# Fewer warm-up products, ScalarE's conversion steps queued behind relus, and the last bank scaled from PSUM

## The chip, the core and the metric

The kernel runs on one NeuronCore of a Trainium2 chip. Five engines each work through an instruction stream of their own, in order: TensorE (PE, with its weight loads shown as PEld), VectorE (DVE), ScalarE (ACT), GpSimd (POOL) and SyncE (SP), which here only issues transfers. They wait for each other by semaphores. The metric is the device time of one execution in microseconds.

## What is computed

Attention over 8 batches, 8 heads, 576 positions and 64 columns per head, with a threshold below the maximum, and then a feed-forward block on the result with a residual:

```python
scores = scale * np.matmul(q, k.transpose(0, 1, 3, 2))
thresh = np.max(scores, axis=-1, keepdims=True) - tau
scores = np.where(scores >= thresh, scores, -1000000000.0)
attn = np.exp(scores - np.max(scores, axis=-1, keepdims=True))
attn = attn / (np.sum(attn, axis=-1, keepdims=True) + 1e-09)
x = np.matmul(attn, v)            # then heads side by side: (8, 576, 512)
mu = np.mean(x, axis=-1, keepdims=True)
var = np.mean((x - mu) ** 2, axis=-1, keepdims=True)
xn = (x - mu) / np.sqrt(var + 1e-06) * g_ln
out = x + np.maximum(xn @ w_ch1, 0.0) @ w_ch2
```

w_ch1 (512 by 2048) and w_ch2 (2048 by 512) come as 64-bit floats, read by the kernel as 64-bit integers; q, k and v are 32-bit floats.

## The kernel before

**Slots.** The attention runs in slots n = 0, 1, ...: nine to a batch (SLOTS), four head pairs by the first 256 query columns, one for the last 64 columns of all heads, four more head pairs. In a slot PE makes the scores (L413) in two banks groups sc0 and sc1; DVE takes the negated maxima (L427), POOL the thresholds (L431), ACT the exponentials (L441, two per bank group), DVE compares, masks and sums (L448). In batch 0 ACT makes diagonal matrices of the reciprocals (L462) and PE turns the weights with them (tp, tr), copied to SBUF by ACT as em and er (L498, L521); from batch 1 on POOL divides (L464), DVE transposes 32 by 32 blocks into et (L538), and SP stores them to a scratch (scr) and reads them back turned. PE multiplies with v (L596, L606), ACT copies to x (L619), POOL sums features (L648). DVE also turns q and k of the slot ahead (turn, L364 to L374), after POOL has scaled q (L360).

**The feed-forward block** has 16 groups g of 288 tokens. Its steps are a generator that is advanced in the four quarters of each slot by `second_part`, which deals PE work by a count of what is owed until the next group. `first_part` computes 16 tiles of hidden units (d = 0 to 15): four products of two halves each into a bank p1, then a relu on ACT (L790). There are two banks for p1 and everything else in that pool, so tile d + 2 waits for the relu of tile d. Meanwhile ACT squares the centred input (L796), POOL adds the four parts (L798), PE multiplies the sum for the variance, and ACT takes log and exponential for the reciprocal root (L806 to L808); DVE refines it (L731 to L735). Group 0 then goes through `second_plain`: for each m = 0 to 3, sixteen products and a copy by ACT (L828). The later groups go through `second_quarters`, seven segments of products on halves of the tokens and of the hidden units, whose banks ACT copies out (L877), and DVE or POOL adds (L881), multiplies by the root and adds x (`finish`, L889 and L881).

**The order is written out by hand.** No scheduler moves instructions: the program order of each engine is the order of the calls. Calls meant for a later place are kept in lists (aside, stores, drops, at_quarter).

**The weights' conversion.** Class `Weights` takes 32 chunks of 128 by 512 (512 KB as 64-bit): 16 of w_ch1, then 16 of w_ch2. SP fetches a chunk into free room (L255). `begin` issues two DVE steps (L274, L278) and two ACT steps (L282 on the low words, L286 squares the high words). `carry` is an integer add on POOL that needs L282 and L278 (L292). `mask` is a DVE step (L301) that needs the carry and L286. `scale` multiplies a chunk of w_ch1 by g on POOL (L313). The first part may not use a tile of w_ch1 until its chunks have been scaled, the second not a tile of w_ch2 until its chunk has been masked. BEGUN says how many chunks have begun by each of three places in a slot. Chunks 12 to 31 begin in slots 6 to 10, when group 0 runs on PE. The rooms are lent from tensors that are not yet used, among them w2, hidden, et, x_room and stage.

**The start.** `constants` multiplies a constant by the identity on PE, with nobody reading the result: 22 products of two halves ahead of the first scores, 26 or 8 ahead of the next four.

**The end.** The last group has no slots left beside it. Its outputs are turned by DVE (`store`, L714) and sent by `send` (L721): four transfers of 36 KB for each of m = 0 to 3, in pieces of 128 bytes. SP sends them all, but in the last group every second one is ACT's.

Of the kernel before, what the change touches and what calls it, by code (L numbers as in the profile page):

```python
# [8 lines left out]
F32 = mybir.dt.float32  # L9
U32 = mybir.dt.uint32  # L10
I32 = mybir.dt.int32
# [7 lines left out]
def kernel(  # L19
# [158 lines left out]
    class Weights:  # L178
# [13 lines left out]
        def __init__(self):  # L192
            self.chunks = [
                (w1_sb[i][:, c : c + WC], w_ch1[i * 128 : (i + 1) * 128, c : c + WC], i)
                for c in range(0, DF, WC)
                for i in range(NK)
            ] + [
                (
                    w2_sb[:, m, d : d + 4].rearrange("p d c -> p (d c)"),
                    w_ch2[d * 128 : (d + 4) * 128, m * 128 : (m + 1) * 128].rearrange(  # L200
                        "(d p) c -> p d c", p=128
                    ),
                    None,
                )
                for m in range(NK)
                for d in range(0, ND, 4)
            ]
            self.n1 = NK * (DF // WC)
            self.fetched = self.begun = self.carried = self.masked = self.scaled = 0
            self.raw, self.made, self.ticks = {}, {}, 2  # L210
            flat = lambda t: t.rearrange("p a b -> p (a b)")

            x_room = ffn.tile([128, NK, TOK], F32, tag="x", bufs=3, name="x_room")
            stage = self.stage = consts.tile([128, 8, WC], F32, name="stage")
            et = att.tile([128, NB, 128], F32, tag="et", bufs=1, name="et0")

            n1 = self.n1  # L220
            self.free = []
            for t, n, before in (
                (w2_sb.rearrange("p m d c -> p (m d) c"), ND // 2, lambda p: n1 + 2 * p),
                (hidden, 4, lambda p: 10),
                (et, 2, lambda p: 2 * n1),
                (x_room, 1, lambda p: 2 * n1),
                (stage, 4, lambda p: 2 * n1),
            ):
                for p in range(n):
                    self.free.append((before(p), -1, flat(t)[:, p * 2 * WC : (p + 1) * 2 * WC]))  # L230
# [34 lines left out]
        def begin(self):  # L265
            i = self.begun
            got = self.piece(i, 1) or self.piece(i, -1)
            if got is None:
                return
            self.made[i] = got  # L270
            a, y = got[2][:, :WC], got[2][:, WC:]
            self.begun += 1
            au, hi = a.bitcast(U32), self.words(i, U32)[:, :, 1]
            nc.vector.tensor_scalar(  # L274
                out=au, in0=hi, scalar1=3, scalar2=0x3FFFFFFF,
                op0=ALU.logical_shift_left, op1=ALU.bitwise_and,
            )
            nc.vector.scalar_tensor_tensor(  # L278
                out=au, in0=hi, scalar=0xC0000000, in1=au,
                op0=ALU.bitwise_and, op1=ALU.bitwise_or,  # L280
            )
            nc.scalar.activation(  # L282
                self.words(i, I32)[:, :, 0], self.words(i, U32)[:, :, 0],
                func=AF.Copy, scale=2.0**-29,
            )
            nc.scalar.activation(y, self.words(i, F32)[:, :, 1], func=AF.Square)  # L286

        def carry(self):
            i = self.carried
# [40 lines left out]
                    break  # L330

        def carry_all(self):
            while self.carried < self.begun:
                self.carry()

# [381 lines left out]
    def send(g, m, ot):  # L717
        b, t = divmod(g, 2)
        for i in range(4):
            f = m * 128 + 32 * i  # L720
            (nc.scalar if g == NG - 1 and i % 2 else nc.sync).dma_start(  # L721
                out=out[b, t * TOK : (t + 1) * TOK, f : f + 32].rearrange(
                    "(n r) c -> r n c", r=32
                ),
                in_=ot[32 * i : 32 * i + 32].rearrange("p (n c) -> p n c", c=32),
            )
# [43 lines left out]
    def first_part(g):  # L770


        xc = centred.pop(g)
        rb = sq = None
        plain = g == 0
        sums_of = differences() if g == 1 else iter(())
        for d in range(ND):
            while conversion.ended < 4 * (d // 4 + 1):
                yield 0, 0
            while d == ND - 2 and len(rooted) <= g:  # L780
                run_all(aside)
            p1 = ps_ff.tile([128, TOK], F32, tag="ff", name="p1")
            for c in range(NK):
                product(
                    p1, lhsT=w1_sb[c][:, d * 128 : (d + 1) * 128], rhs=xc[:, c],
                    start=(c == 0), stop=(c == NK - 1),
                )
                if c < NK - 1:
                    yield 1, 1
            nc.scalar.activation(hidden[:, d], p1, func=AF.Relu)  # L790
            next(sums_of, None)
            yield 2, 1
            if sq is None and d and (plain or part > 1 or d == ND // 2 - 1):
                squared = d
                sq = hidden[:, ND - NK :]
                nc.scalar.activation(sq, xc, func=AF.Square)  # L796
                for c in range(1, NK):
                    nc.gpsimd.tensor_tensor(out=sq[:, 0], in0=sq[:, 0], in1=sq[:, c], op=ALU.add)  # L798
            elif sq is not None and rb is None and (
                d >= squared + (7 if plain else 3) and part > (0 if plain else 1)  # L800
                or d == ND - NK - 1
            ):
                var = ps_ff.tile([128, TOK], F32, tag="ff", name="var")
                product(var, lhsT=avg_sb, rhs=sq[:, 0], start=True, stop=True)
                rb = ffn.tile([128, TOK], F32, tag="rb", bufs=2, name="rb")
                nc.scalar.activation(sq[:, 2], var, func=AF.Identity, bias=eps_sb)  # L806
                nc.scalar.activation(rb, sq[:, 2], func=AF.Ln)
                nc.scalar.activation(rb, rb, func=AF.Exp, scale=-0.5)  # L808
                aside.append(lambda: root(rb, sq[:, 2], sq[:, 3]))
                yield 1, 1  # L810
        for _ in sums_of:
            pass
        return rb
# [18 lines left out]
    def second_quarters(g, rb):  # L832
# [13 lines left out]
        def later(*calls, urgent=None):  # L846
            for what, cost, fn, eng, *args in calls:

                def go(what=what, fn=fn, eng=eng, args=args):
                    fn(eng, *args)  # L850
                    done.add(what)

                drops.append((urgent, now, eng, cost, go))
# [7 lines left out]
                at = (slice(None), slice(d, d + 4))  # L861
                eng.tensor_tensor(out=out[at], in0=in0[at], in1=in1[at], op=op)  # L862

        def segment(weights, rhs, out=None):
            bank = ps_ff.tile([128, HM, HT], F32, tag="ff", name="seg")
            for d in range(HD):
                for m in range(HM):
                    at, end = (d, m), (HD - 1, HM - 1)
                    product(
                        bank[:, m], lhsT=weights[:, m, d], rhs=rhs[:, d],  # L870
                        start=at == (0, 0), stop=at == end,
                    )
                    if at != end:
                        yield 2, 0.5
            if out is None:
                out = ffn.tile([128, HM, HT], F32, tag="part", bufs=4, name="part")
            nc.scalar.copy(out, bank)  # L877
            return out

        def add(eng, out, a, b):  # L880
# [39 lines left out]
            ("22", 1, add, dve, y22, y21, p5), ("21", 1, add, dve, y21, y21, p4),  # L920
            ("hi", 3, finish, done_by, 1),
        )
        if g == NG - 1:
            later(*((f"o{m}", 1, store, dve, g, m, y[:, m]) for m in (2, 3)))
        yield 2, 0.5
        last = segment(s4, b22)
        for _ in range(12):
            yield next(last)
        banks_taken[0] = False
        while waiting_mean:  # L930
            mean_of(waiting_mean.pop(0))
        p3 = yield from last
        later(("12", 1, add, dve, y12, y12, p3), ("done12", 2, finish, done_by, 0, 1))
        later(
            *((f"o{m}", 1, store, dve, g, m, y[:, m]) for m in ((2, 3, 0, 1) if g < NG - 1 else (0, 1)))
        )
# [22 lines left out]
    def run(n, i):  # L959
        for fn, args in later_calls.pop((n, i), ()):  # L960
            fn(*args)
# [69 lines left out]
    def constants(times):  # L1031

        warm = ps_ff.tile([128, QH], F32, tag="ff", name="warm")
        for _ in range(times):
            product(warm[:, :128], lhsT=avg_sb, rhs=ident, start=True, stop=True)

    constants(22)
    turn(0)
    for n in range(NS):
        b, s = divmod(n, SLOTS)  # L1040
# [7 lines left out]
        rest = exponentials(n)  # L1048
        es, thr = next(rest)
        run(n, 0)  # L1050
        if n >= HP:
            conversion.fetch(3)
        run_first(stores)
# [13 lines left out]
            run_all(aside)  # L1067
        conversion.mask_all()
        conversion.begin_to(masks_at)
        conversion.carry_all()  # L1070
        conversion.scale_all()
        run(n, 1)
        second_part(n, 1)
        blocks_go = by_blocks(b * HP)
        diags = weights(es, thr, blocks_go)
        run_all(aside)
# [84 lines left out]
```

## Time and profile before

| | |
|---|---|
| Median of 3 runs | 1362.81 us (1362.71 to 1362.99) |
| Profiled execution: its time, its span | 1362.91 us, 1361.1 us |
| PE busy, share of the span | 1329.7 us, 98% |
| DVE, POOL, ACT busy | 873.6, 614.2, 469.9 us |
| Mean granted clock of TensorE | 0.998 |
| Last product of PE ends | 1351.3 us |

The span runs from the first to the last instruction of the core. A line of a timeline has start, duration, engine, line, operation, output and input by the program's names, shape and count, and in brackets how long the engine was idle before it and what released it. A line of waits has who waited for whom, the total, how often and the longest. In PE's lines two records stand for each product of a half. A transfer's line with SPq, ACTq or POOLq is its issue by that engine's queue, not the movement of the data; the landing is given apart. The chain is followed back from the last instruction, at each step to what released it.

### The profile page before, as it was taken

The page shows a single profiled execution, that of the slowest core. Times are in us where ns is not written, and L with a number is a line of the kernel's source. Part 1 is how long each engine was busy: PE and PEld are TensorE (multiplying, and loading weights), DVE is VectorE, ACT ScalarE, POOL GpSimd, SP SyncE. Part 2 cuts the span into 40 slices and gives each one's busy share as a digit, 9 for nine tenths or more (in the row PEclk, how much of TensorE's full clock was granted, in tenths as well). Part 3 has the DMA queues.
Part 4 walks back from the last instruction along what each step waited for, and adds up shares of the span by engine and source line. Part 5 has one row for each costly group of instructions (what it writes and reads, how often), then busy time and mean ns, then how long its engine had stood idle before and what let it go on. Part 6 is the DMA issues. An engine that isn't in the chain of part 4 may idle for free.

```text
span 1361.1 us, 40915 instructions
## 1 busy us (share of the span) xinstructions
PE 1329.7 (98%) x17648; PEld 1005.7 (74%) x17648; DVE 873.6 (64%) x1530; ACT 469.9 (35%) x1023; POOL 614.2 (45%) x820
## 2 busy tenths in 40 slices
PE   8989999999999999999999999999999999999997
PEld 7756667869687686867768696876869677786967
DVE  6986967766755676666766667556766667665202
ACT  4866533232323323232333323233232323333120
POOL 3554545444534444444533545444444445344311
PEclk9999999999999999999999999999999999999999
DMA  8822475457644666437744576446754376443211
GB/s 173 249 63 88 96 205 159 144 165 199 185 149 145 184 183 186 148 121 193 202 129 162 143 203 179 150 145 185 193 174 153 122 197 177 140 159 132 63 19 19
DMA packets 322084, 206.88 MB, mean 152 GB/s; under 512 B 248048, under 2 KB 279536, under 8 KB 313840
## 3 DMA queue, kind: packets, MB, share of 16 engines
q1 hardware_dynamic: 314704, 203.38, 51.4%
q8 instruction: 138, 2.26, 0.7%
q10 hardware_dynamic: 7168, 0.89, 0.5%
q14 instruction: 42, 0.34, 0.1%
q0 software_dynamic: 32, 0.00, 0.0%
HBM read 120.46 MB, written 83.76 MB: 150 GB/s over the span
## 4 chain that ended last, share of the span: by engine, by line
PE 89%; DVE 4%; ACT 3%; POOL 1%; issue 1%; DMA 0%; ACTq 0%; DVEq 0%; POOLq 0%; SPq 0%
PE p L101 36%; PE seg L101 30%; PE sc L413 10%; PE sc L596 8%; PE sc L606 2%; PE tp L101 1%; DVE e L448 1%; ACT e L441 1%; DVE w L301 1%; PE var L101 1%; PE mean L101 0%; DMA x_room<-in_moe_w_ch_dram 0%; ACT em L498 0%; DVE w L278 0%; ACT part L877 0%
## 5 line engine op out<-in xcount | busy, mean ns | idle before, releaser
L101 PE MATMUL p<-xc,w 128*64 128x288 f32 x4096 | 517.9, 408 | 11.5 <-ACT part L877 4.6
L101 PEld LDWEIGHTS p<-xc,w 128*64 128x64 f32 x4096 | 287.1, 137 | 219.8 <-issue 15.0
L427 DVE TENSOR_REDUCE neg<-sc 128x2 f32<-128x1152 f32 x144 | 188.6, 1352 | 287.2 <-PE sc L413 286.8
L464 POOL TENSOR_SCALAR e<-e,den 128x576 f32<-128x576 f32 x252 | 194.0, 781 | 133.8 <-DVE den L453 133.8
L101 PE MATMUL seg<-hidden,w 128*64 128x144 f32 x3840 | 247.9, 287 | 0.0
L101 PEld LDWEIGHTS seg<-hidden,w 128*64 128x64 f32 x3840 | 234.9, 137 | 11.5 <-issue 8.6
L448 DVE SCALAR_TENSOR_TENSOR e<-sc,thr,e 128x576 f32<-128x576 f32 x288 | 222.1, 809 | 20.5 <-POOL thr L431 11.7
L790 ACT ACTIVATE hidden<-p 128x288 f32<-128x288 f32 x256 | 106.4, 416 | 309.1 <-PE p L101 309.1
L431 POOL TENSOR_SCALAR thr<-neg,low_sb 128x2 f32<-128x2 f32 x144 | 41.8, 290 | 376.0 <-DVE neg L427 375.8
L441 ACT ACTIVATE e<-sc,neg 128x576 f32<-128x576 f32 x288 | 197.8, 754 | 3.9 <-DVE neg L427 3.9
L538 DVE STREAM_TRANSPOSE et<-e 128x1152 f32<-128x1152 f32 x112 | 153.3, 1374 | 14.4 <-POOL e L464 13.7
L413 PE MATMUL sc<-kT,qT 64*64 64x384 f32 (+3 forms) x2048 | 139.4, 403 | 1.8 <-DVE e L448 1.7
L596 PE MATMUL sc<-em,v_in 128*64 128x128 f32 (+1 forms) x2368 | 129.5, 263 | 0.0
L596 PEld LDWEIGHTS sc<-em,v_in 128*64 128x64 f32 x2368 | 122.8, 137 | 7.9
L101 PE MATMUL seg<-hidden,stage 128*64 128x144 f32 x1920 | 123.3, 286 | 0.0
L101 PEld LDWEIGHTS seg<-hidden,stage 128*64 128x64 f32 x1920 | 117.6, 137 | 2.9 <-issue 2.9
L619 ACT COPY x<-sc 128x128 f32<-128x128 f32 x120 | 31.7, 266 | 239.7 <-PE sc L413 171.9
L862 POOL TENSOR_TENSOR hidden<-hidden 128x576 f32<-128x576 f32 x60 | 84.8, 1428 | 51.9 <-ACT hidden L790 42.3
L413 PEld LDWEIGHTS sc<-kT,qT 64*64 64x64 f32 x2048 | 76.2, 133 | 42.7 <-issue 21.2
L877 ACT COPY part<-seg 128x288 f32<-128x288 f32 x75 | 30.3, 403 | 196.7 <-PE seg L101 190.0
L862 DVE TENSOR_TENSOR hidden<-hidden 128x576 f32<-128x576 f32 x60 | 51.2, 887 | 51.5 <-PE seg L101 48.5
L101 PE MATMUL seg<-hidden,e 128*64 128x144 f32 x960 | 65.3, 286 | 0.0
(143 smaller groups left out, 1101.3 us busy)
## 6 DMA issues: line engine op xcount, KB each, us to landing
scr<-et SPq DMA_DIRECT2D x63, 1152.0 KB, 5.0
em<-scr SPq DMA_DIRECT2D x63, 1024.0 KB, 5.8
q_in<-in_q_dram SPq DMA_DIRECT2D x124, 72.0 KB, 2.6
out_dram<-ot SPq DMA_DIRECT2D x248, 36.0 KB, 3.8
k_in<-in_k_dram SPq DMA_DIRECT2D x120, 72.0 KB, 2.8
er<-scr SPq DMA_DIRECT2D x126, 64.0 KB, 5.1
v_in<-in_v_dram SPq DMA_DIRECT2D x28, 256.0 KB, 5.4
w<-in_moe_w_ch_dram SPq DMA_DIRECT2D x12, 512.0 KB, 4.9
```

The source lines that it names most:

```text
L101: nc.tensor.matmul(out[r], lhsT=lhsT[:, r], rhs=rhs, **flags)
L413: nc.tensor.matmul(sc[h][64 * i : 64 * i + 64, at : at + n], lhsT=ql[r] if s == HP else qT[r, half, j * 128 + 64 * i : j * 128 + 64 * i + 64],
L427: nc.vector.tensor_reduce(out=neg[:, i], in_=pairs[h], axis=AXL.X, op=ALU.max, negate=True,)
L431: nc.gpsimd.tensor_scalar(out=thr[:, i], in0=neg[:, i], scalar1=-1.0, scalar2=low_sb, op0=ALU.mult, op1=ALU.add,)
L441: nc.scalar.activation(es[:, i], blocks[i], func=AF.Exp, bias=neg[:, i : i + 1])
L448: nc.vector.scalar_tensor_tensor(out=es[:, i], in0=blocks[i], scalar=thr[:, i : i + 1], in1=es[:, i], op0=ALU.is_ge, op1=ALU.mult, accum_o ...
L464: nc.gpsimd.tensor_scalar(out=es[:, i], in0=es[:, i], scalar1=den[:, i : i + 1], scalar2=1.0, op0=ALU.mult, op1=ALU.mult,)
L538: nc.vector.transpose(et[:, :, 64 * h : 64 * h + 64].rearrange("p n (j c) -> p j n c", j=2), es[:, 2 * h : 2 * h + 2].rearrange("p j (n c) ...
L596: nc.tensor.matmul(dst[64 * h : 64 * h + 64], lhsT=vt[:, h, c, :], rhs=pick(em[:, 2 * j : 2 * j + 2, c], h), start=c == 0 and first, stop= ...
L619: nc.scalar.copy(x_of(2 * b + (s > HP))[:, s % (HP + 1), 128 * j : 128 * j + 128], pv[j])
L790: nc.scalar.activation(hidden[:, d], p1, func=AF.Relu)
L862: eng.tensor_tensor(out=out[at], in0=in0[at], in1=in1[at], op=op)
```

## The change

It has three parts. First, `constants(22)` becomes `constants(14)`. Second, the two ACT steps of `begin` are not issued at once but put on a list, `on_scalar`; `first_part` takes one from the list after each relu (`flush(1)`), and `carry_all` takes all that are left. In slots from 6 on, the carries and scales of quarter 1 come after that quarter's feed-forward work, no longer ahead of it; in slot 6 the second pair of exponentials is issued ahead of quarter 0's. Third, in the last group the final bank is not copied by ACT but multiplied by the root by DVE, from PSUM; the rest of that quarter is finished before (`done12` ahead), and the two are added. The stores of m = 2 go to SP, those of m = 3 to POOL (gpsimd), those of m = 0 and 1 alternate between SP and ACT.

```diff
-            self.raw, self.made, self.ticks = {}, {}, 2
+            self.raw, self.made, self.ticks, self.on_scalar = {}, {}, 2, []
...
-            nc.scalar.activation(
-                self.words(i, I32)[:, :, 0], self.words(i, U32)[:, :, 0],
-                func=AF.Copy, scale=2.0**-29,
-            )
-            nc.scalar.activation(y, self.words(i, F32)[:, :, 1], func=AF.Square)
+            low, low_in, hi_in = self.words(i, I32), self.words(i, U32), self.words(i, F32)
+            self.on_scalar += [
+                lambda: nc.scalar.activation(
+                    low[:, :, 0], low_in[:, :, 0], func=AF.Copy, scale=2.0**-29
+                ),
+                lambda: nc.scalar.activation(y, hi_in[:, :, 1], func=AF.Square),
+            ]
+
+        def flush(self, most=99):
+            while self.on_scalar and most:
+                most -= 1
+                self.on_scalar.pop(0)()
...
         def carry_all(self):
+            self.flush()
             while self.carried < self.begun:
                 self.carry()
...
-            (nc.scalar if g == NG - 1 and i % 2 else nc.sync).dma_start(
+            eng = nc.sync
+            if g == NG - 1:
+                eng = (nc.sync, nc.gpsimd)[m % 2] if m >= HM else (nc.sync, nc.scalar)[i % 2]
+            eng.dma_start(
...
             nc.scalar.activation(hidden[:, d], p1, func=AF.Relu)
+            conversion.flush(1)
...
+        def times_root(out, bank):
+            r = rb[:, late].unsqueeze(1).to_broadcast([128, HM, HT])
+            dve.tensor_tensor(out=out, in0=bank, in1=r, op=ALU.mult)
+
-        def segment(weights, rhs, out=None):
+        def segment(weights, rhs, out=None, as_it_is=False):
...
-            nc.scalar.copy(out, bank)
+            if as_it_is:
+                times_root(out, bank)
+            else:
+                nc.scalar.copy(out, bank)
...
-        if g == NG - 1:
+        ends_here = g == NG - 1
+        if ends_here:
+            later(("done12", 2, finish, dve, 0, 1))
             later(*((f"o{m}", 1, store, dve, g, m, y[:, m]) for m in (2, 3)))
         yield 2, 0.5
-        last = segment(s4, b22)
+        last = segment(s4, b22, as_it_is=ends_here)
...
-        later(("12", 1, add, dve, y12, y12, p3), ("done12", 2, finish, done_by, 0, 1))
+        later(("12", 1, add, dve, y12, y12, p3))
+        if not ends_here:
+            later(("done12", 2, finish, done_by, 0, 1))
...
-    constants(22)
+    constants(14)
...
         run(n, 0)
+        if n == HP + 2:
+            next(rest, None)
...
-        conversion.carry_all()
-        conversion.scale_all()
-        run(n, 1)
-        second_part(n, 1)
+        if n <= HP + 1:
+            conversion.carry_all()
+            conversion.scale_all()
+        run(n, 1)
+        second_part(n, 1)
+        conversion.carry_all()
+        conversion.scale_all()
```

## The prediction

> **What bounds the kernel now.** I read the busy line first, then busy time by stretch, then PE's waits, the chain that ended last, and the timelines of the places that the diff touches. Busy times and stretches (columns: stretch, its length, then busy us of PE, PEld, DVE, ACT, POOL with their instructions, the granted clock, the share of the DMA engines, GB/s):
>
> ```profile
> PE 1329.7 (98%) x17648; PEld 1005.7 (74%) x17648; DVE 873.6 (64%) x1530; ACT 469.9 (35%) x1023; POOL 614.2 (45%) x820
> ...
> 0.00:85.00 85.00, 76.80 (x1210) 62.84 (x1212) 70.55 (x136) 55.99 (x117) 40.41 (x62) 1.00 0.76 194
> 85.00:190.00 105.00, 96.59 (x1046) 62.16 (x1044) 78.94 (x140) 57.63 (x118) 49.42 (x53) 1.00 0.38 98
> 190.00:348.00 158.00, 157.37 (x2146) 120.32 (x2146) 107.84 (x185) 49.59 (x109) 82.85 (x106) 1.00 0.58 172
> ```
>
> From 190 to 1351 us PE is idle 0.6 in 158: nothing but fewer products helps there, and a gain or loss ahead of it is carried to the end whole. So the change is decided in three places: the start, 85 to 190 (PE idle 8.4), and the 9.8 us behind PE's last product. PE's waits between 85 and 190 (total, times, longest):
>
> ```profile
> PE p L101 <- ACT hidden L790: 4.1, 3, 1.5
> PE p L101 <- ACT hidden L806: 1.7, 1, 1.7
> PE tp L101 <- ACT em L498: 1.2, 2, 0.7
> ```
>
> The timelines of ACT and PE show the first of them: the relu that frees a bank stands behind exponentials, four conversion steps and a square, though its product ended near 89.4.
>
> ```profile
> 87.88 1.37 ACT L441 ACTIVATE e<-sc,neg 128x576 f32<-128x576 f32 x2
> 89.13 0.70 ACT L282 ACTIVATE w<-w 128x512 int32<-128x512 uint32 x1
> ...
> 91.44 1.16 ACT L796 ACTIVATE hidden<-xc 128x1152 f32<-128x1152 f32 x1
> 92.49 0.41 ACT L790 ACTIVATE hidden<-p 128x288 f32<-128x288 f32 x1
> ...
> 92.95 2.16 PE L101 MATMUL p<-xc,w 128*64 128x288 f32 x16 [1.54 <-ACT hidden L790]
> ```
>
> But the chain (start, us, what) is not PE's from 136 to 184: it runs through POOL and DVE to the fetch of the last chunk.
>
> ```profile
> 169.85 0.37 DVE ot L714
> ...
> 170.34 6.52 DMA x_room<-in_moe_w_ch_dram
> ...
> 184.17 6.53 PE p L101 x52
> ```
>
> **Part 1, constants(22) to (14).** Gone are 8 products of two halves, 32 records of 88. The timeline of PE and the issue of g_sb, which part 3 needs (KB, us to landing):
>
> ```profile
> 2.37 7.43 PE L101 MATMUL warm<-ident,avg_sb 128*64 128x128 f32 x88 [2.37 <-POOL ident masks.py:199]
> 9.72 2.17 PE L413 MATMUL sc<-kT,qT 64*64 64x384 f32 x32
> ...
> g_sb<-in_moe_g_ln_dram POOLq DMA_DIRECT2D x1, 2.0 KB, 4.3
> ```
>
> The scores need DVE's qT, two transposes from 7.76 to 8.72, so they wait for the warm products. Later, 104 such records take 5.90, 57 ns each. If the first x ran at half that speed, 114x + 57(88-x) = 7430 gives x = 42, so the step lies at 2.37 + 42·0.114 = 7.2 us; records per us do rise from 14 to 20 and more at 7. The 56 records that stay end at 7.2 + 14·0.057 = 8.0. The Trainium skill (TensorE: Matmul & The Clock Gate, Part 1) says the slow budget is some 3.4 us of time, not a number of matmuls; the trace has about 4.8. By either the remaining 5.6 us outlast it. Had they not, the first scores would take twice their 2.1: a loss of 2.1 instead of a gain. (The page's granted clock is 1.00 all through and shows no step.) The scores start at 8.77 if they wait for both transposes, at 8.3 if for the first: gain 0.95 to 1.4. DVE is busy from there to 85 with gaps under 1 us, and the chain there has no DMA, so I carry 1.0; 0.3 if the early transfers (0.76 of the engines) take it back.
>
> **Part 2, the conversion behind the relus.** The instructions of PE and DVE keep their order (but for the tail); ACT's change from slot 6 on, POOL does three L798 adds ahead of two carries. Nothing is added: each chunk still has two ACT steps of 0.57 (start to start) and one POOL carry of 1.3.
>
> Slot 6: the second exponentials move into ACT's idle 1.99 before 85.63. DVE's third mask (3.58 of waiting for them) need not wait. Relu d=1 at 87.57, square to 89.15, relu d=2 at 89.55: PE's d=4 starts at 91.4, not 92.95. Four conversion steps (2.3) and four diags (1.16) come next, so relu d=3 is at 93.4 and d=5 at 93.85 instead of 96.66: 2.8 ahead. DVE's next masks need POOL's carries, which wait for the adds (89.2 to 92.3): DVE is done at about 102, the scores of slot 7 come at 102.0 and DVE's maximum at 104. No loss.
>
> Slot 7: the 1.74 wait goes, since the three variance steps (1.35) now stand ahead of four conversion steps. Those and the diags (3.5) then hold relu d=10 to 117.3, so d=12 starts at 117.65 for 122.80: PE is about 5.0 ahead.
>
> Slots 8 and 9 decide what of this stays. Moving a step later on ACT makes its carry late on POOL, and DVE's masks behind it. Chunks 26 and 27 now convert behind the copy L828, which waits for PE's end of m=0 (142.0): carries at 143.0 and 144.3, DVE's masks L301 at 146 and 147.5. Before, these two took 3.00 us from 149.53 where two alone take 1.25, beside a carry at 149.47; I keep such collisions. DVE's maximum of slot 9 comes at about 151.7 for 155.98: 4.3 ahead. Chunk 30 waits for L828 of m=1 (159.1): carry at 160.1, and POOL's four L464 queue behind it; DVE's et transposes need those and end 3.1 to 4.3 earlier than 169.8. SP issues scr, then chunk 31, in order: that far ahead does the last fetch start, and 13.8 us later (184.17 - 170.34) PE gets it. PE arrives 5 ahead and waits a microsecond or so for mask L301. I take 3.7; upper end 5.0 (PE's whole lead), lower end 1.0 (two more carries of 1.3 in DVE's way).
>
> **Part 3, the tail.** DVE and ACT before:
>
> ```profile
> 1352.03 1.92 ACTq L721 DMA_DIRECT2D out_dram<-ot  x4
> 1354.06 0.40 ACT L877 COPY part<-seg 128x288 f32<-128x288 f32 x1 [6.21 <-DMA out_dram<-ot]
> ...
> 1354.49 0.46 DVE L881 TENSOR_TENSOR y<-y,part 128x288 f32<-128x288 f32 x1 [2.14 <-ACT part L877]
> ```
>
> PE ends at 1351.3, but the copy stands behind four stores on ACT. After: DVE ends its big product and sum at 1351.48, then two of 0.49 (done12), transposes of m=2,3 to 1353.36 (before 1352.36), the new product from PSUM (no row; 0.5 as the SBUF form, 0.4 to 0.8), the add, transposes to 1355.35 instead of 1356.87: 1.5. SP and ACT then issue their last by 1357.0 for 1358.45. The open term is POOL: four stores of m=3 from 1353.4. At g_sb's 0.95 an issue the fourth starts at 1356.25. The Trainium skill (DMA: Bandwidth & Descriptors, Anatomy of one DMA — SWDGE path) puts such a transfer at 2.0 us plus bytes/436e3: landing by 1358.3 if that counts from the issue, so SP sets the end and the tail gains 1.45. The row says 4.3: landing 1360.55, against 1359.9 before (1357.98 + 1.9): loss 0.65. It was taken while tau_sb on SP took 2.8; stores in the tail take 1.8, so I take 3.3: 1359.55, gain 0.35. POOL has been idle since 1343.8.
>
> **Sum.** 1.0 + 3.7 + 0.35 = 5.05. The profiled execution took 1362.91 (span 1361.1 and 1.8 around it), the median is 1362.81, 0.10 lower; I take the sum from the median: 1357.8.
>
> **Rivals.** A: all of PE's lead gets through and POOL's stores land early: 1.2 + 5.0 + 1.3 = 7.5, 1355.3. For it: the chunk chain's collisions were bad before and might fall better. Against: chunk 30's order. B: the wait moves instead of going; the fetch of chunk 31 leaves only 1 us earlier, early transfers take half of part 1, POOL's landing takes the tail: 0.5 + 1.0 - 0.3 = 1.2, 1361.6. For it: the chain of before is DVE's and POOL's there, and PE waited 0.27 on the mask at 184.17 already. C, slower: POOL's stores cost far more to issue than g_sb. q0 shows 32 packets: 16 for a semaphore (as 7168 on ACT's queue is 8·576 + 8·288 + 16·16), so g_sb was 16 packets and each store is 288. At p us an issue the end is 1353.4 + 4p + 2.35 (3.3 less one issue) + 1.2 (1361.1 less 1359.9). Against the other gains of 4.7 it costs over 0.2% from p = 2.9 on; at 3.5 the time is 1368. That part 2 does nothing is excluded by ACT's order: the waits of 1.54 and 1.74 stand right behind steps that move.
>
> **How the numbers follow.** Likeliest 0.56 (its own range 1356.0 to 1359.8), A 0.18, B 0.18, C 0.08. The range goes from A's 1355.2 to B's 1361.6 and leaves out C and the ends of A. A measurement tells 0.2%, 2.7 us, from no change: faster 0.74, same 0.18, slower 0.08.
>
> **What would show it.** First scores at 8.3 to 8.8; PE's waits on L790 and L806 between 85 and 125 near 1.2 instead of 5.8; slot 8's scores near 122.7 (all with part 1's 1.0 off); a wait of 1 us or so on mask L301 near 179; the chunk 31 fetch near 165.5; DVE's last transposes 1.5 nearer to PE's end, and POOL's four issues 0.95 each. Wrong: issues of 2 us and more, a fetch of chunk 31 after 168, or new waits of PE behind 190.

## The result, and the profile after

The changed kernel takes 1357.64 us, the median of seven runs (1357.24 to 1359.45), against 1362.81 before (1362.31 to 1363.43, seven runs): a ratio of 0.9965, 95% interval [0.9954, 0.9977], so 5.2 us or 0.35% faster. The profiled execution took 1357.61 with a span of 1355.8, for 1362.91 and 1361.1 before. Lines of the code have moved: the relu L790 is now L801, the square L796 L808, ACT's conversion L282 and L286 are L284 and L287, POOL's carry L292 is L299, DVE's mask L301 L308, `send` L721 L732.

The busy line and busy time by stretch of the changed kernel (columns as before):

```profile
PE 1326.8 (98%) x17616; PEld 1003.3 (74%) x17616; DVE 874.0 (64%) x1531; ACT 470.0 (35%) x1022; POOL 615.3 (45%) x824
...
84.00:186.00 102.00, 96.91 (x1056) 62.88 (x1054) 80.31 (x139) 57.51 (x118) 50.30 (x54) 1.00 0.39 101
186.00:344.00 158.00, 157.38 (x2146) 120.10 (x2144) 106.97 (x185) 48.94 (x109) 81.71 (x105) 1.00 0.58 174
```

The work is the same, but for the 32 records of PE and, in the tail, a copy of ACT that is now DVE's product and four issues of POOL's. Behind 186 us PE runs as before, idle 5.0 us in all up to its last product in both kernels: the products of the tile that needs the last chunk begin at 179.22 for 184.17, and PE's last product ends at 1346.33 for 1351.33. All of the 5.0 us on PE come from ahead of that tile. In 84 to 186 PE is idle 5.1 us, for 8.4 in the stretch shown of before. Its largest waits from 80 to 186 us (three of five lines):

```profile
PE tp L101 <- ACT em L506: 2.1, 3, 0.8
PE p L101 <- DVE w L308: 1.4, 1, 1.4
PE p L101 <- ACT hidden L801: 1.1, 2, 0.7
```

The 5.8 us on relus and the variance are 1.1; the wait on a mask was 0.3 and is 1.4. The waits on em are as before, 1.9 from 81 us on. The timeline of ACT in the place shown of before:

```profile
82.34 1.39 ACT L449 ACTIVATE e<-sc,neg 128x576 f32<-128x576 f32 x2
...
88.32 0.41 ACT L801 ACTIVATE hidden<-p 128x288 f32<-128x288 f32 x1 [0.48 <-PE p L101]
88.63 0.68 ACT L284 ACTIVATE w<-w 128x512 int32<-128x512 uint32 x1
...
92.11 0.39 ACT L801 ACTIVATE hidden<-p 128x288 f32<-128x288 f32 x1
```

PE's products that waited for ACT in slots 6 and 7 before, behind the one of d = 4 at 92.95 that is shown above, and those that still wait now:

```profile
96.66 2.65 PE L101 MATMUL p<-xc,w 128*64 128x288 f32 x20 [1.55 <-ACT hidden L790]
...
117.70 4.10 PE L101 MATMUL p<-xc,w 128*64 128x288 f32 x32 [1.74 <-ACT hidden L806]
122.80 2.65 PE L101 MATMUL p<-xc,w 128*64 128x288 f32 x20 [0.99 <-ACT hidden L790]
```

```profile
92.55 1.68 PE L101 MATMUL p<-xc,w 128*64 128x288 f32 x12 [0.40 <-ACT hidden L801]
...
116.47 2.65 PE L101 MATMUL p<-xc,w 128*64 128x288 f32 x20 [0.73 <-ACT hidden L801]
```

The exponentials stand at 82.34 in a gap, and the relu of d = 2 (88.32) is done in time, so the wait of d = 4 is gone. Only the relu of d = 3 (92.11) is behind four conversion steps and the diags: d = 5 waits 0.40 instead of 1.55. In slot 7 the wait for the variance is gone, and d = 12 waits 0.73 instead of 0.99.

The chain from 158 to 179 us (start, us, what):

```profile
158.57 1.29 POOL et L299
159.87 0.28 POOL e L472
...
165.37 6.55 DMA x_room<-in_moe_w_ch_dram
...
176.58 0.73 POOL q_in L368
177.33 0.77 DVE qT L376 x2
...
178.59 0.59 DVE w L308
...
179.22 6.53 PE p L101 x52
```

Chunk 30's carry is at 158.57, POOL's divisions queue behind it, and the last fetch leaves at 165.37 for 170.34. It is still what PE waits for at 179.22, but not by the conversion alone: the carry of chunk 31 is done at 174.6, and its mask stands on DVE behind transposes of q, which wait for POOL.

The start on PE, DVE's wait for the third k, and the tail on DVE and the issuing queues, first two lines of the tail before and then the changed kernel:

```profile
1356.03 0.84 DVE L714 STREAM_TRANSPOSE ot<-y 128x288 f32<-128x288 f32 x2
1356.54 1.91 ACTq L721 DMA_DIRECT2D out_dram<-ot  x4
```

```profile
2.36 4.88 PE L101 MATMUL warm<-ident,avg_sb 128*64 128x128 f32 x56 [2.36 <-POOL ident masks.py:199]
8.20 2.17 PE L421 MATMUL sc<-kT,qT 64*64 64x384 f32 x32 [0.96 <-DVE qT L381]
...
23.70 0.78 DVE L372 STREAM_TRANSPOSE kT<-k_in 128x576 f32<-128x576 f32 x1 [0.89 <-DMA k_in<-in_k_dram]
...
1347.76 5.46 SPq L732 DMA_DIRECT2D out_dram<-ot  x8
1348.01 0.42 DVE L878 TENSOR_TENSOR part<-seg,rb 128x288 f32<-128x288 f32 x1
1348.39 2.50 POOL L732 DMA_DIRECT2D out_dram<-ot  x4 [9.63 <-DVE ot L722]
...
1349.01 0.84 DVE L722 STREAM_TRANSPOSE ot<-y 128x288 f32<-128x288 f32 x2
1349.52 2.33 ACTq L732 DMA_DIRECT2D out_dram<-ot  x4
```

The scores start 1.5 earlier. At 23.7 DVE waits 0.89 for the third head pair's k, as it did not in the profiled execution before, and PE has 1.2 of the 1.5 left at the fourth slot (41.57 for 42.75). In the tail DVE is done 3.5 us behind PE's last product for 5.5 before. Yet the span ends 9.47 behind it, for 9.77: two microseconds on DVE became 0.3 at the end.

### The profile page after: what moved, and what is told of

The parts are those of the page before. It is cut to its first block, busy times and chain, and to the rows that moved or that the text cites. A ratio compares the mean times of both kernels' runs of the same rounds, so it can differ in the third digit from the quotient of the medians.

```text
span 1355.8 us, 40852 instructions
## 1 busy us (share of the span) xinstructions
PE 1326.8 (98%) x17616; PEld 1003.3 (74%) x17616; DVE 874.0 (64%) x1531; ACT 470.0 (35%) x1022; POOL 615.3 (45%) x824
## 4 chain that ended last, share of the span: by engine, by line
PE 90%; DVE 3%; ACT 2%; DMA 1%; POOL 1%; issue 1%; SPq 1%; POOLq 0%; DVEq 0%; ACTq 0%
PE p L101 37%; PE seg L101 30%; PE sc L421 10%; PE sc L604 8%; PE sc L614 2%; PE tp L101 1%; ACT e L449 1%; DVE e L456 1%; PE var L101 1%; PE mean L101 1%; SPq L118 0%; DMA x_room<-in_moe_w_ch_dram 0%; ACT em L506 0%; DMA qk_room<-in_q_dram 0%; DVE w L308 0%
## 5 line engine op out<-in xcount | busy, mean ns | idle before, releaser
L435 DVE TENSOR_REDUCE neg<-sc 128x2 f32<-128x1152 f32 x144 | 188.6, 1351 | 280.8 <-PE sc L421 280.2
L801 ACT ACTIVATE hidden<-p 128x288 f32<-128x288 f32 x256 | 106.6, 417 | 303.6 <-PE p L101 303.6
```

The source lines that it names most:

```text
L435: nc.vector.tensor_reduce(out=neg[:, i], in_=pairs[h], axis=AXL.X, op=ALU.max, negate=True,)
```

## The experiments

Each kernel was timed with runs of the kernel before on the same chip; "gain" is the difference of the two medians (before: 1362.62, 1362.87, 1362.60 and 1363.02 in the four groups). The 95% intervals of the ratios reach 0.08% to 0.17% to either side, 1.2 to 2.3 us: for a difference of 1 us, the place in the trace says more than the times.

### The three parts alone

**Part 1 alone.**

```diff
-    constants(22)
+    constants(14)
```

> The kernel before with constants(14) for constants(22) alone. Theory (the three parts add up): first scores at 8.2 us, the attention of batch 0 stays 1.0 to 1.2 us ahead, and so does the end: 1361.6 to 1361.8 us. Rival (the lead is lost at the fetch of the last weight chunk, which waits for transfers): below 0.5 us of gain, 1362.3 or more.

1362.41 us (ten runs, 1362.05 to 1365.35), a gain of 0.2; ratio 1.0004 [0.9995, 1.0013]. The profiled execution shows 1.1 at the first scores (8.65 for 9.72) and 0.74 at the last chunk's tile (183.43), and DVE's wait for k:

```profile
24.19 0.78 DVE L364 STREAM_TRANSPOSE kT<-k_in 128x576 f32<-128x576 f32 x1 [0.91 <-DMA k_in<-in_k_dram]
```

So the lead isn't lost at the last chunk, as the rival had it, since the fetch leaves 0.72 sooner too. It is lost in part at the third head pair. What it is worth in time this run can't tell from nothing: three of the ten runs lie 2.3 to 2.9 us above the median, where none of the 28 of the kernel before in this group lies more than 0.9 above its own, so by the means (1363.11 for 1362.66) part 1 alone is slower, if by less than the interval.

**Part 2 alone**: the changed kernel with the 22 products and the tail of before.

> The changed kernel with constants(22) and the old tail: ScalarE's part of the chunks behind the relus alone. Theory: 3.8 us faster than before (1359.0), PE about 5.1 ahead at the scores of slot 8 and then waiting about 1.4 for the mask of chunk 31. Rival (PE's whole lead stays): 5 us, 1357.7.

1358.85 us (eight runs, 1358.28 to 1359.60), a gain of 3.8; ratio 0.9973 [0.9963, 0.9984]. The last chunk's tile begins at 180.20, 3.97 ahead of before, with a wait of 1.32 on its mask. This is most of the change, and the size that the prediction gave this part.

**Part 3 alone**: the kernel before with the changed tail.

> The kernel before with the new tail alone (last bank multiplied from PSUM, stores of m=3 by GpSimd, of m=2 by SyncE). Theory: 0.3 us faster, 1362.5, with SyncE's last two stores held about 1.8 us. Rival (the tail is worth what DVE's shorter chain shows): 1.5 us, 1361.3.

1362.43 us (ten runs, 1361.69 to 1363.14), a gain of 0.2; ratio 0.9999 [0.9989, 1.0008]. The span ends 9.5 behind PE's last product (1351.70 to 1361.2), as in the changed kernel. The tail gains next to nothing even when nothing else is changed. The three parts alone sum to 4.2 us by the medians, for 5.2 together; by the traces they sum to 5.0 (0.74, 3.97 and 0.3). The intervals allow for the difference.

### The start: speed and transfers

**Four products instead of fourteen.**

```diff
-    constants(14)
+    constants(4)
```

> The changed kernel with constants(4). Theory (the first products run at half speed for a time of about 4.8 us of PE work, not for a number of products): the 16 records end near 4.2 us, the first scores still start at 8.2 but at half speed, 4.2 us instead of 2.1: 2 us slower than the changed kernel, 1359.7. Rival (the half speed is a start-up time that passes whether PE works or not): scores at 8.2 take 2.1 us, no change, 1357.6.

1359.17 us (nine runs, 1358.98 to 1359.38), a gain of 3.5 for the 5.2 of the changed kernel; ratio 0.9974 [0.9965, 0.9984]. PE's timeline:

```profile
2.37 1.98 PE L101 MATMUL warm<-ident,avg_sb 128*64 128x128 f32 x16 [2.37 <-POOL ident masks.py:199]
8.27 3.98 PE L421 MATMUL sc<-kT,qT 64*64 64x384 f32 x32 [3.92 <-DVE qT L381]
```

The scores begin where they did with 14 but take 3.98 instead of 2.17: the products' use is that the scores meet PE at full speed, and fourteen are still enough for that, four are not. That was the condition of part 1. A start-up that passes whether PE works or not, the rival, is excluded: PE was idle for 3.9 us ahead of these scores, and they still ran at half speed, until 12.2 us.

**The third k ahead of the third q.**

```diff
-        for i, (name, src) in enumerate((("q", q), ("k", k))):
+        for i, (name, src) in ((0, ("q", q)), (1, ("k", k)))[:: -1 if u == 2 else 1]:
```

> The changed kernel with the third head pair's k loaded ahead of its q (its room is free 1.35 us sooner than q's: DVE has turned k at 13.7 and q at 15.05). Theory (the late k takes 0.35 of part 1's lead in most executions and 2.5 or more in some, because the clock falls while PE waits): DVE's wait of 0.9 on k at 23.7 goes or is halved, slot 3's scores come at 41.2 instead of 41.57, the median is 1357.3 and no run lies over 1.2 us above it. Rival (the early transfers share one rate, so what is gained on k is lost on q, which POOL has to scale): scores of slot 3 at 41.6 or later, 1357.6 or more, and some runs at 1359 and above.

1358.08 us (seven runs, 1357.48 to 1361.00), a gain of 4.5; ratio 0.9969 [0.9958, 0.9980]. The theory falls. DVE's timeline:

```profile
22.75 0.77 DVE L372 STREAM_TRANSPOSE kT<-k_in 128x576 f32<-128x576 f32 x1
24.86 0.78 DVE L381 STREAM_TRANSPOSE qT<-q_in 128x256 f32<-128x256 f32 x2 [1.34 <-POOL q_in L368]
```

The wait for k is gone and one of 1.34 for the scaled q is there in its place; the fourth slot's scores come at 42.08 instead of 41.57. SP needs 3.6 and 4.5 us to issue the two loads, and whichever is second is late: this change of order moved the wait and did not shorten it. Nor is the wait part 1's alone. In the kernels with 22 products that were profiled DVE waits for this k 0 us (before), 0.27 (part 2 alone), 0.82 (the last section of experiments) and 0.99 (part 3 alone), with 14 in the order of the change 0.89 to 1.46, and 2.58 in one execution. Leaving that one out, the first scores are 1.2 apart in the mean (8.32 for 9.54) and those of the fourth slot 0.8 (41.94 for 42.75).

### The middle: exponentials and the last fetch

**Without the early second exponentials in slot 6.**

```diff
-        if n == HP + 2:
-            next(rest, None)
```

> The changed kernel without the earlier second exponentials of slot 6. Theory (the end of the conversion is set by the chain to chunk 31, with PE 1.4 us ahead of it): PE's lead at slot 8 shrinks by up to 1.3 us, its wait for the mask of chunk 31 shrinks too, and the time changes by less than 0.7 us. Rival (each us that PE loses in slot 6 is lost at the end): 1.3 us slower, 1358.9.

1359.12 us (nine runs, 1358.33 to 1361.64), a gain of 3.8 for 5.2; ratio 0.9975 [0.9965, 0.9985]. ACT's and PE's timelines:

```profile
86.93 1.37 ACT L449 ACTIVATE e<-sc,neg 128x576 f32<-128x576 f32 x2
88.18 1.17 ACT L808 ACTIVATE hidden<-xc 128x1152 f32<-128x1152 f32 x1
89.23 0.42 ACT L801 ACTIVATE hidden<-p 128x288 f32<-128x288 f32 x1
...
93.45 2.65 PE L101 MATMUL p<-xc,w 128*64 128x288 f32 x20 [1.06 <-ACT hidden L801]
```

The pair is back behind the relu of d = 1, the relus of d = 2 and 3 are 0.9 late, PE waits 1.06 instead of 0.40, and the last chunk's tile begins at 180.34, 1.1 later (0.2 of that from this execution's start). These two lines are worth some 0.9 of part 2's 3.8. The theory falls and the rival is the nearer: PE's wait on the last mask did not shrink (1.35 for 1.37), since the last fetch left 1.1 later too (166.51 for 165.37). The chain to chunk 31 moves with PE and gives no slack.

**The last chunk fetched ahead of the scratch store.**

```diff
+        if n == SLOTS:
+            conversion.fetch(3)
         if blocks_go:
             scr = turn_blocks(s, es)
```

> The changed kernel with the fetch of the last weight chunk (31) issued by SyncE in slot 9 ahead of the store of the turned weights (scr) instead of behind it. Theory (PE's wait of 1.4 us near 178 us is set by that fetch): the fetch starts near 159 instead of 165.4, the wait goes, 1.2 to 1.4 us faster than the changed kernel, 1356.3. Rival (DVE's and GpSimd's work of slot 10 sets the mask whatever the fetch does): the wait stays, 1357.6.

1356.73 us (four runs, 1356.69 to 1360.00), a gain of 6.1; ratio 0.9959 [0.9944, 0.9974]. PE's wait on the mask falls from 1.37 to 0.19. The profiled execution is the one of 1360.00, which lost some 3 us around the third head pair's k (shown in the last section), but the wait is the same in the kernel with both faults mended, whose execution was not held up so and whose fetch leaves at 159.98 instead of 165.37:

```profile
178.70 2.16 PE L101 MATMUL p<-hidden,w 128*64 128x288 f32 x16 [0.19 <-DVE w L308]
```

So the last fetch does hold PE in the changed kernel, for about 1 us.

### The tail: who sends

**SP and ACT alternating as before**, the product from PSUM kept.

```diff
-            eng = nc.sync
-            if g == NG - 1:
-                eng = (nc.sync, nc.gpsimd)[m % 2] if m >= HM else (nc.sync, nc.scalar)[i % 2]
-            eng.dma_start(
+            (nc.scalar if g == NG - 1 and i % 2 else nc.sync).dma_start(
```

> The changed kernel with the last group's stores on SyncE and ScalarE in turn, as before; the last bank is still multiplied from PSUM. Theory (the gain of DVE's chain is eaten by stores waiting for earlier stores to land, and GpSimd's stores have a part in that by their slow landing): without them the last stores go out by about 1.5 us after DVE's last transpose and the tail is 0.5 to 1.2 us shorter than in the changed kernel, 1356.8. Rival (GpSimd's queue takes load off the others): ScalarE and SyncE have eight stores each, the tail is 0.3 or more longer, 1358.0.

1356.67 us (four runs, 1356.51 to 1356.76, all below the fastest of the changed kernel), a gain of 6.2; ratio 0.9953 [0.9936, 0.9969]. Its tail's timeline, and the landing times of its stores (min, median, max), then those of the changed kernel:

```profile
1348.11 3.87 SPq L729 DMA_DIRECT2D out_dram<-ot  x8
1348.11 3.98 ACTq L729 DMA_DIRECT2D out_dram<-ot  x8
```

```profile
DMA to landing us min/median/max: 1.7/1.9/2.1
```

```profile
DMA to landing us min/median/max: 1.6/2.4/3.7
```

The span ends 8.2 behind PE's last product (1346.67 to 1354.9) for 9.5. Both queues are done issuing at 1352.1, 5.4 behind PE's last product, without POOL's help. Moving stores to POOL costs 1.2 us of the 1.5 that DVE's earlier end brings.

**Whole outputs to one queue**: m = 0 to ACT, m = 1 to SP, m = 2 to SP and m = 3 to POOL as changed.

```diff
-                eng = (nc.sync, nc.gpsimd)[m % 2] if m >= HM else (nc.sync, nc.scalar)[i % 2]
+                eng = (nc.sync, nc.gpsimd)[m % 2] if m >= HM else (nc.scalar, nc.sync)[m % 2]
```

> The changed kernel with the stores of m=0 all on ScalarE and those of m=1 all on SyncE, instead of each m on both in turn. Theory (SyncE's last two stores are held 1.8 us by ScalarE's stores of m=0, which land late): with no turns between the two, SyncE's four stores of m=1 go out at once after DVE's transpose, by 1351.9 instead of 1353.2: 0.5 to 1.2 us faster than the changed kernel, 1356.8. Rival (any late landing holds them, whichever queue it is on): no change, 1357.6.

1358.33 us (five runs, 1357.47 to 1360.83), a gain of 4.5; ratio 0.9968 [0.9955, 0.9981]; the span ends 9.3 behind PE. In the changed kernel SP's last two stores wait 1.8 us for an earlier store to land; here that wait is 1.0 at most and the end is hardly nearer. So it isn't this wait that holds the end; the next kernel has none of it.

**Only m = 3 on POOL.**

```diff
-                eng = (nc.sync, nc.gpsimd)[m % 2] if m >= HM else (nc.sync, nc.scalar)[i % 2]
+                eng = nc.gpsimd if m == 3 else (nc.sync, nc.scalar)[i % 2]
```

> The changed kernel with the stores of m = 2 alternating between SP and ACT; only those of m = 3 stay POOL's. Theory (with m = 2 on SP alone the transfers of the tail begin at half their rate, 74 GB/s for about 1.5 us against 135 to 145 GB/s with two queues, and the span ends with the transfers): the first stretch is back at 135 GB/s, the span ends 8.2 to 8.7 behind PE's last product, and the median is 1356.7 to 1357.0. Rival (POOL's four stores are the cost, by their issue of 0.62 each and by slowing the other queues' landings to 3 us and more): the tail stays near 9.4 and the median at 1357.6 or above.

1357.88 us (five runs, 1357.46 to 1358.23), a gain of 5.1; ratio 0.9961 [0.9948, 0.9975]. The theory of a half-used start falls: with m = 2 on two queues again, nothing is won. Timeline and landings of its stores:

```profile
1348.47 3.66 SPq L732 DMA_DIRECT2D out_dram<-ot  x6
1348.47 3.82 ACTq L732 DMA_DIRECT2D out_dram<-ot  x6
...
1349.11 2.49 POOL L732 DMA_DIRECT2D out_dram<-ot  x4 [9.64 <-DVE ot L722]
```

```profile
DMA to landing us min/median/max: 1.7/2.3/3.6
```

All queues are done issuing by 1352.3, 5.3 behind PE's last product, as with the old queues, and no queue waits for a store. But SP's and ACT's stores now land a median of 2.6 and 2.8 us after issue instead of 1.8 and 2.0, and the span ends 9.3 behind PE. With POOL's four stores beside them the others land later in each of the three ways they were mixed. Why wasn't tried: a third queue of another engine, or stores by POOL in pieces of another size, would tell whether it is the number of queues or the way POOL sends.

### Both faults mended

**Early fetch and old queues**, with 14 and with 22 constants' products.

> The changed kernel with both faults mended: the fetch of chunk 31 is issued ahead of the scratch store, and the last stores alternate between SP and ACT for every m, as before. Theory (the two waits lie behind one another, so what each gave alone adds): 1357.64 less 0.9 (early fetch, 1356.73 alone) less 1.0 (queues, 1356.67 alone) = 1355.7; PE's wait on the mask of chunk 31 about 0.2, the span's end 8.3 behind PE's last product. Rival (they do not add, a further wait takes the place of one of them): 1356.5 or more. Some runs may lie 2.5 to 3.5 us above the median, as one in four to ten did in the kernels with 14 constants' products.

> The kernel named best with 22 constants' products again, so without part 1. Theory (part 1 is worth the 0.4 to 0.7 that its lead in the trace shows at the fetch of the last chunk, but exposes the start to the transfer of the third head pair's k): median 0.4 to 0.7 above that of best, no wait of DVE on that k beyond 0.3, and no run over 1.5 us above the median. Rival (the runs far above the median have another cause): they are there with 22 as well, one in four to ten. Rival 2 (part 1 is worth nothing): the median within 0.2 of best.

With 14: 1355.85 us (six runs, 1355.22 to 1358.29), a gain of 6.8; ratio 0.9949 [0.9937, 0.9962], and five of the six runs lie below the fastest of the changed kernel (1357.24). With 22: 1356.26 us (six runs, 1355.49 to 1359.10), ratio 0.9952 [0.9941, 0.9964]. The two faults add, as expected (1355.7). Part 1 is worth 0.4 by the medians and 0.43 by the traces at the last chunk's tile (178.70 and 179.13), though the first scores are 1.1 apart; the times alone don't tell it from zero. DVE's wait for the third k is 1.46 with 14 and 0.82 with 22, where 0.3 at most had been expected with 22:

```profile
24.78 0.78 DVE L372 STREAM_TRANSPOSE kT<-k_in 128x576 f32<-128x576 f32 x1 [0.82 <-DMA k_in<-in_k_dram]
```

The far-off runs are not part 1's alone: one is there with 22, and in this group two of eleven runs of the kernel before lie 3 us above its median. But they are more frequent with it: over all groups 8 of 57 runs with 14 products lie 2 us or more above the median of their kernel in its group, and 3 of 92 with 22. What PE waits for next, in the chain of the kernel with 14:

```profile
173.06 1.37 DVE neg L435
...
176.06 0.73 POOL q_in L368
...
176.81 0.77 DVE qT L376 x2
...
178.07 0.58 DVE w L308
...
178.70 6.53 PE p L101 x52
```

No transfer is in it any more: the mask stands behind DVE's transposes of q, these behind POOL's scaling, and that behind a maximum that PE's own scores release. This is why 5 us of an earlier fetch bring only 1.2 of the wait.

## Why the prediction was right, and where it was wrong

The forecast was 1357.8, the result 1357.64, with faster as the likeliest sign. That the two are 0.2 apart is in part luck: part 1 was put 0.3 to 0.6 too high, part 3 came out by errors that offset each other, and the interval is wider than both. But most of its steps can be read off the traces; subtract 1.19 us, PE's lead at 83 us, where the prediction counts without part 1.

- **Where the time is decided.** Right: PE has no new wait behind 190, and a gain ahead of it arrives whole (184.17 less 179.22 is 4.95, PE's last end 5.0 earlier). The 0.6 of idle time holds from 190 to 348 only; up to 1351 it is 5.0 in 1161, nearly all of it waits for the copies of ACT (4.6, the longest 0.6), and it is the same after.
- **Part 2, slots 6 and 7.** Right to a tenth: d = 5 predicted at 93.85, measured 92.55 + 1.19 = 93.74; d = 12 predicted at 117.65, measured 116.47 + 1.19 = 117.66. Waits on relus and variance predicted near 1.2, measured 1.1. That the early exponentials carry 0.9 of it was shown by taking them out.
- **Part 2, what stays of the lead.** Right: predicted 3.7 for the last fetch, measured 170.34 less 165.37 less 1.19, 3.78; part 2 alone brought 3.8. The wait of a microsecond on the last mask was measured as 1.37, and fetching earlier took it down to 0.19. DVE's two masks together again took 2.99, as the step that kept the collision had it.
- **Part 1.** The mechanism was right, a size off: "I carry 1.0". The first scores gained 1.2 in the mean of the traces, since they need only the first of the two transposes, but the next step named the danger and I gave it too little weight: "0.3 if the early transfers take it back". They take a part of it: DVE waits longer for the third k, and 0.4 by the paired kernels, 0.7 at the most by a trace, reaches the last chunk. "The chain there has no DMA" was read in one execution of the kernel before, where k came just in time; others with 22 products waited for it too. The speed of PE was not in danger with 14, and four products showed that it would have been.
- **Part 3.** The sum was right (0.35 predicted, 0.30 measured) by errors that offset each other. "SP and ACT then issue their last by 1357.0" failed: that is 5.7 behind PE's end, and SP was done at 1353.2, 6.9 behind it, where ACT's last issue before was 7.1 behind. And POOL as the queue that sets the end failed: its issues took 0.62, not 0.95, and its stores landed 2.3 to 3.1 after issue (median 2.6), not 3.3. (The Trainium skill, DMA: Bandwidth & Descriptors, Anatomy of one DMA — SWDGE path, has 2.0 us plus bytes/436e3, 2.1 for 36 KB by this estimate, and was nearer than the 4.3 in the row of g_sb.) What held the end were SP's and ACT's stores, which landed late while POOL's moved. I had priced a queue by itself, and not what it does to its neighbours. DVE's part was better than predicted: its last transposes came 2.0 nearer PE's end, not 1.5: each step was a little shorter than reckoned, the product from PSUM 0.42 for 0.5.
- **Rival A** (1355.3) is near what the kernel with both faults mended reached, 1355.85, but by another way: there POOL stores nothing. **Rival B** had one true piece, the transfers against part 1, and a wrong one: the chain of chunk 31 let 3.8 of PE's 5.0 through, not 1. **Rival C** fell with its premise: the software queue shows 160 packets for 32 before, so a store is 32 and not 288, and its issue 0.62 us.

## What to carry to other kernels

When a step is moved behind what the critical engine waits for, follow the moved step's own consumers to the last transfer that they release: here that bounded the gain, and two lines that put the fetch ahead of a store behind it brought a further microsecond. A lead won at the start lasts only until the first transfer that it catches up with, even if the trace before shows no wait on it; look for how much later its consumer came, and at more than one execution. A further queue is not free capacity for the last stores: price it by what happens to the landings of the queues already at work.

## What the runs showed of the hardware

**Stores of SP and ACT land later beside POOL's.** The same sixteen stores of 36 KB landed in 1.7 to 2.1 us from SP and ACT alone. When four of them were POOL's, those of SP and ACT took up to 3.4, 3.6 and 3.7 in the three mixes. POOL's stores appear as 32 packets each (128 for four), ACT's as 304 (1216 for four).

**The start at full speed moves from execution to execution.** The 56 records ahead of the first scores took 4.88 in the changed kernel, 4.60 in part 1 alone and 6.15 with the old queues, where nothing ahead of them differs. By records in half microseconds the step to full speed falls at about 5.6, 5.2 and not before 8.4 us, 3 to 6 us behind the first product. The Trainium skill (TensorE: Matmul & The Clock Gate, Part 1) gives some 3.4 us of time and says that the step varies by 500 ns either way from run to run; here it varies by 3 us. Fourteen products covered all three, the last only just: its scores began at 8.45 and took 2.17.

**The granted clock fell behind two short waits of PE.** In the execution of 1360.00 with the early fetch, DVE waited 2.58 for the third k, and PE 1.47 and 0.61 for DVE. Busy time by stretch (the column ahead of the DMA share is the granted clock), first in that execution, then in the changed kernel:

```profile
28.00:32.00 4.00, 2.52 (x36) 1.61 (x30) 3.96 (x10) 0.86 (x3) 2.27 (x3) 1.00 1.11 153
32.00:36.00 4.00, 3.40 (x32) 1.85 (x34) 3.41 (x7) 2.38 (x6) 1.58 (x2) 0.70 0.71 127
36.00:40.00 4.00, 4.00 (x64) 3.77 (x60) 3.56 (x7) 2.25 (x4) 1.97 (x5) 0.87 0.94 294
```

```profile
32.00:36.00 4.00, 4.00 (x68) 3.43 (x64) 3.63 (x4) 3.10 (x6) 3.17 (x5) 1.00 0.92 257
```

The clock fell to 0.70, 0.50 between 34 and 36 us, and the scores' 28 records took 3.12 instead of 2.16. DVE had the k 2.1 us later than in the changed kernel, 0.4 of that from this execution's first scores, and the fourth slot's scores came 3.7 later (45.29 for 41.57). In the kernel with both faults mended PE waited 0.36 and 0.61 at the same place and the clock stayed at 1.00. One trace shows the fall, and that the waits caused it is only argued from the order; whether the other runs that lie 2 to 3.5 us above their medians have the same cause wasn't profiled.
